# The mirrored rows of x, read backwards by plain transfers with the two halves of each third swapped

## The chip, the cores and the metric

The kernel runs on one core of a Trainium2 chip. The metric is device time in microseconds (us). Before the change the median of three runs is 629.89 us (629.77 to 629.99). The profiled execution took 629.88 us; the span that the profile covers is 628.1 us of it.

The engines of the core are named as in the profile: PE (matrix products), PEld (loads of the matrix that stays in PE), DVE, ACT and POOL (elementwise work), and SP, which only issues transfers. "SPq", "ACTq" and "POOLq" are issues and waits of an engine's instruction queue. Transfers run on 16 DMA engines.

## The reference

A two-dimensional Fourier transform of x, of which the real part is kept, goes through a gated feed-forward layer:

```python
X = np.fft.fft(x, axis=1)          # x: (8, 3008, 256)
X = np.fft.fft(X, axis=2)
x = X.real.reshape(8 * 3008, 256)
gate = np.maximum(x @ w_gate, 0.0) # 256 -> 1536
val = x @ w_val
out = gate * val @ w_out           # 1536 -> 256
```

## The kernel before, in words

With S = 3008 rows, D = 256 channels and H = S/2 = 1504, the transform along the rows is written with cosines and sines, and rows s and S - s are added or subtracted first. So each batch is loaded twice. **XD** holds rows in rising order: partition p of third t, slot q, half r of the sequence holds row 1 + 256 t + 2 p + q (+ r H). **XG** holds, on the same partitions, the pairs of rows that mirror these, in falling order. A third has 128 partitions (t = 0, 1) or 120 (t = 2), and row 0 sits beside them on partition 120 of t = 2 (`load_mirror_0`).

*How the mirrored rows come in.* For batch 0 the first third is read upwards (`load_upward`) and turned by products with a matrix `turned` (`turn`, L393, products L395); the other thirds, and all of batch 1, are fetched by a gather on POOL with an index per partition (`load_mirror`, L118). From batch 2 on, `reverse(b)` (L176) copies the rows backwards from x into a scratch tensor `xr` in DRAM, in six blocks of 64 rows, `reverse_0` (L182) adds row 0, and `load_reversed` (L186) reads `xr` into XG.

*The folds.* In batch 0, DVE adds XD and XG into AA, third by third (L461 to L478), and forms F and G. For every later batch POOL does it in `fold_steps` (L224): six `fold_a` (L198) add XD into XG, six `fold_pq` (L206) combine the halves into AA, then `fold_f` and `fold_g` write F and G. XG is free for the next batch when `fold_pq` and `small` (L251) are done. The folds of batches 1 and 2 run in one piece in batch 0 (`run_fold(99)`); those of batch b + 2 for b = 1 to 5 are spread over the tiles of batch b, 0.72 us of them for each tile.

*The tiles.* Each batch goes through PE in blocks of columns (four of 376 in batch 0, three of at most 512 later), and each block through 12 tiles of 128 hidden units. From batch 1 on, one tile (`slot`, L1030) takes a product for the sine part (L1016), its copy by ACT (L1019), a seed of the cosine part by ACT from the row block CB (L1011), a sum on DVE (L1027), a sum on POOL (L1028), the value products and the gated product h on DVE (L909). POOL executes L1028 and the fold steps in the order in which they are written. The output products (L781) of one block are spread over the tiles of the next, ACT copies each finished pair of output banks to `os` (L794, four buffers), and SP stores it to `out` (L806).

*SP's order.* SP issues in the order in which the program writes it: loads of XD (L96, L102), of XG, of CB and V, the copies of leftover columns (LB, L904), and the stores. An instruction of SP that waits holds back all behind it. `channel_loads` (L128) fetch one channel of batches 2 to 7 with 4-byte elements, into CX; `channel_turn` (L143) puts the mirrored part into a scratch tensor in DRAM backwards (L151, two blocks of 64 or 60 rows) and gets it back (L155). `wrow` and `brow` (L835, L836) carry a row of weights through DRAM to the bias of the seeds (`b2`, L837).

*The start.* SP and ACT issue the first loads, POOL and DVE build small vectors, PE and ACT build the tables of angles (`angle`, L357), POOL issues the loads of the weights (`load_w`, L341) on its software queue, and PE then transforms batch 0 (`dft_first`, L612, products L621) as its folds come in. The first tile's first product is L964.

Of the kernel before, what the change touches and what calls it, by code (L numbers as in the profile page):

```python
# [11 lines left out]
F32 = mybir.dt.float32  # L12
# [14 lines left out]
ROUND = 12582912.0  # L27
# [7 lines left out]
def kernel(  # L35
# [55 lines left out]
    pairs = x.rearrange("b (s two) d -> (b s) (two d)", two=2)  # L91

    def load_rows(b, ts=range(3)):
        for t in ts:
            n = (128, 128, 112)[t]
            nc.sync.dma_start(out=XD[0:n, :, t].rearrange("p r a d -> p r (a d)"),  # L96
                              in_=dram(x, (b * S + 1 + t * 256) * D, [[2 * D, n], [H * D, 2], [1, 2 * D]]))

    def load_last(b):
        for a in range(2):  # L100
            n = (8, 7)[a]
            nc.sync.dma_start(out=XD[112:112 + n, :, 2, a, :], in_=dram(x, (b * S + 1 + 2 * (256 + 112) + a) * D, [[2 * D, n], [H * D, 2], [1, D]]))  # L102
# [9 lines left out]
    def load_half(t, r, queue):  # L112
        queue.dma_start(out=XD[:, r, t], in_=dram(x, (1 + r * H + t * 256) * D, [[2 * D, 128], [D, 2], [1, D]]))

# [3 lines left out]
    def load_mirror(b, t, r):  # L118
        n = (128, 128, 120)[t]
        nc.gpsimd.indirect_dma_start(  # L120
            out=XG[0:n, r, t, :, :].rearrange("p a d -> p (a d)"), out_offset=None, in_=pairs,
            in_offset=bass.IndirectOffsetOnAxis(ap=gidx[0:n, 2 * t + r:2 * t + r + 1], axis=0), element_offset=b * S * D)

    def load_upward(t, r, queue):
        first = H - 128 - 128 * t - r * (H // 2)
        queue.dma_start(out=XG[:, r, t, :, :].rearrange("p a d -> p (a d)"), in_=pairs[first:first + 128, :])

    def channel_loads():  # L128
# [5 lines left out]
        for t in range(2):  # L134
            load(CX[:, 0, t], 2 * S + 1 + 256 * t, [2 * D, 128], [D, 2])
            load(CX[:, 1, t], 3 * S - H - 256 - 256 * t, [2 * D, 128], [D, 2])
        for q in range(2):
            load(CX[0:120 - q, 0, 2, q], 2 * S + 513 + q, [2 * D, 120 - q])
        load(CX[120:121, 0, 2, 1], 2 * S, [2 * D, 1])
        load(CX[0:120, 1, 2], 3 * S - H - 512 - 240, [2 * D, 120], [D, 2])  # L140
        return loads

    def channel_turn():  # L143
# [3 lines left out]
        for k, (ts, h, w) in enumerate(pieces):  # L147
# [5 lines left out]
            def get(ts=ts, h=h, cr=cr):  # L153
                for c in range(2):
                    nc.sync.dma_start(out=CX[c * h:c * h + h, 1, ts].rearrange("p t q n -> p (t q n)"), in_=cr[1 - c])  # L155
# [16 lines left out]

    PC, NC = 64, 6
    xr = nc.dram_tensor("xr", (B, 2, NC, PC, 2 * D), F32).ap()

    def reverse(b):  # L176

        for r in range(2):
            top = (H - 1 - r * (H // 2)) - NC * PC + PC
            nc.sync.dma_start(out=xr[b, 1 - r], in_=dram(x, b * S * D + top * 2 * D, [[PC * 2 * D, NC], [-2 * D, PC], [1, 2 * D]]))  # L180

    def reverse_0(b):  # L182
        for r in range(2):
            nc.sync.dma_start(out=xr[b, 1 - r, 0, 120 - PC:121 - PC, :], in_=dram(x, b * S * D + r * H * D, [[2 * D, 1], [1, 2 * D]]))

    def load_reversed(b):  # L186
        W = PC * 2 * D
        for h in range(2):
            nc.sync.dma_start(out=XG[h * PC:(h + 1) * PC].rearrange("p r t a d -> p (r t) (a d)"),
                              in_=dram(xr, (b * 2 * NC + 2 * NC - 1 - h) * W, [[2 * D, PC], [-2 * W, NC], [1, 2 * D]]))  # L190

# [32 lines left out]
    def fold_steps(b):  # L224
# [14 lines left out]
        if b + 1 < B:  # L239
            steps.append((0.0, lambda: reverse_0(b + 1) if b else None))  # L240
# [18 lines left out]
        if b + 1 < B:  # L259
            last.insert(3, (0.0, lambda: load_reversed(b + 1)))  # L260
# [956 lines left out]
```

## Time and profile before

| | us |
|---|---|
| median of three runs | 629.89 |
| profiled execution | 629.88 |
| its span | 628.1 |
| PE busy | 617.9 |
| DVE busy | 550.9 |
| POOL busy | 502.7 |
| ACT busy | 445.8 |

A row of a timeline is: start in us, duration in us, engine, source line, operation, output <- inputs, shapes, how many instructions were merged, and in brackets how long the engine was idle before and what released it. A row of the table by stretches is: its bounds, its length, then the busy time of PE, PEld, DVE, ACT and POOL with their numbers of instructions, the granted clock, the mean share of the 16 DMA engines and the GB/s that they moved. A share can exceed 1, since the records of packets in flight on one engine overlap. A group of a line or tile gives the number of instructions and the least, median and largest duration in ns.

### The profile page before, as it was taken

To read this page: it belongs to the slowest core of one execution; us is meant where nothing else is said; L and a number is where in the kernel's file an instruction comes from. 1 tells how busy PE (TensorE), PEld (TensorE's weight loads), DVE (VectorE), ACT (ScalarE), POOL (GpSimd) and SP (SyncE) were. 2 spreads that over 40 slices of the span, in tenths; PEclk is the share of its full clock that TensorE was granted. 3 is DMA by queue.
4 is the path that set the end of the run, shared out by engine and by line. 5 is a ranking of instruction groups with operands and counts; after the bars stand their busy time and mean duration, and the time that the engine had idled before them with its cause. 6 is when DMAs were issued, how large, how long until landed. Compare 5 with 4: busy or idle time off the path is not lost.

```text
span 628.1 us, 12374 instructions
## 1 busy us (share of the span) xinstructions
PE 617.9 (98%) x4057; PEld 398.2 (63%) x4102; DVE 550.9 (88%) x979; ACT 445.8 (71%) x814; POOL 502.7 (80%) x478
## 2 busy tenths in 40 slices
PE   8999999999999999999999999999999999999997
PEld 3566666666666666666666666666666666666666
DVE  8886676999899899988999999899999989999991
ACT  7796667777677767777777767777777777777762
POOL 8988992998899988799979989699886566666660
PEclk9999999999999999999999999999999999999999
DMA  9954758734263427315362326211221111211113
GB/s 240 210 201 130 169 184 106 186 66 141 86 155 137 132 70 196 101 48 161 91 185 68 131 76 138 61 52 35 76 62 37 42 60 56 60 35 50 53 50 95
DMA packets 84465, 66.47 MB, mean 106 GB/s; under 512 B 40070, under 2 KB 67494, under 8 KB 84400
## 3 DMA queue, kind: packets, MB, share of 16 engines
q1 hardware_dynamic: 79814, 60.01, 34.5%
q0 software_dynamic: 3984, 4.92, 4.0%
q8 instruction: 32, 0.52, 0.4%
q10 hardware_dynamic: 602, 0.75, 0.3%
q14 instruction: 33, 0.27, 0.1%
HBM read 41.88 MB, written 34.17 MB: 121 GB/s over the span
## 4 chain that ended last, share of the span: by engine, by line
PE 93%; DVE 3%; issue 1%; ACT 1%; DMA 1%; DVEq 0%; ACTq 0%
PE o L781 37%; PE v L874 10%; PE v L879 10%; PE g L1016 8%; PE p L1023 8%; PE v L873 8%; PE d L585 4%; DVE h L909 2%; PE p L879 1%; PE p L873 1%; PE p L874 1%; PE v L395 1%; DMA XG<-in_x_dram 1%; DVE h L898 1%; DVE r L1027 1%
## 5 line engine op out<-in xcount | busy, mean ns | idle before, releaser
L1028 POOL TENSOR_TENSOR r<-r 128x512 f32<-128x512 f32 (+1 forms) x251 | 312.8, 1252 | 100.0 <-DVE r L1027 98.9
L909 DVE SCALAR_TENSOR_TENSOR h<-r,v 128x512 bf16<-128x512 f32 (+1 forms) x502 | 317.3, 673 | 39.1 <-PE v L879 25.5
L781 PE MATMUL o<-wo,h 128*128 128x256 bf16 x2172 | 330.7, 273 | 0.0
L781 PEld LDWEIGHTS <-h 128*128 128x128 bf16 x2220 | 216.4, 97 | 112.7 <-issue 1.6
L1011 ACT ACTIVATE p<-CB,b 128x512 f32<-128x512 bf16 (+1 forms) x251 | 171.7, 684 | 73.5 <-DVE r L1027 72.6
L1019 ACT COPY r<-g 128x512 f32<-128x512 f32 (+1 forms) x251 | 144.8, 577 | 65.4 <-PE g L1016 56.8
L1027 DVE SCALAR_TENSOR_TENSOR r<-r,p 128x512 f32<-128x512 f32 (+1 forms) x251 | 168.1, 670 | 0.6 <-ACT r L1019 0.6
L874 PE MATMUL v<-V,WB 128*128 128x512 bf16 (+3 forms) x296 | 108.7, 367 | 2.2
L879 PE MATMUL v<-V,WM 128*128 128x512 bf16 (+1 forms) x252 | 94.4, 375 | 1.1 <-DVE h L909 0.7
L1016 PE MATMUL g<-V,WM 128*128 128x512 bf16 (+1 forms) x251 | 94.2, 375 | 0.2
L1023 PE MATMUL p<-U,WA 128*128 128x512 bf16 (+1 forms) x251 | 94.2, 375 | 0.0
L873 PE MATMUL v<-U,WA 128*128 128x512 bf16 (+3 forms) x254 | 92.7, 365 | 0.0
L898 DVE TENSOR_TENSOR h<-r,v 128x376 bf16<-128x376 f32 (+2 forms) x90 | 46.0, 546 | 17.3 <-PE v L879 9.1
L873 PEld LDWEIGHTS <-WA 128*128 128x128 bf16 x348 | 33.9, 97 | 39.9 <-issue 10.7
L874 PEld LDWEIGHTS <-WB 128*128 128x128 bf16 x348 | 33.9, 97 | 33.7 <-ACT WB L677 0.2
L794 ACT COPY os<-o 128x512 f32<-128x512 f32 x92 | 52.6, 571 | 3.5 <-issue 3.0
L198 POOL TENSOR_TENSOR XG<-XG,XD 128x510 f32<-128x510 f32 x42 | 52.9, 1267 | 0.6 <-DMA XG<-xr 0.6
L889 ACT ACTIVATE r<-p 128x376 f32<-128x376 f32 (+1 forms) x80 | 38.0, 486 | 17.8 <-PE p L879 9.6
L206 POOL TENSOR_TENSOR AA<-XG 128x510 f32<-128x510 f32 x42 | 45.3, 1089 | 0.0
L1016 PEld LDWEIGHTS <-WM 128*128 128x128 bf16 x251 | 24.5, 98 | 5.7 <-issue 0.3
L879 PEld LDWEIGHTS <-WM 128*128 128x128 bf16 x253 | 24.7, 98 | 3.1
L1023 PEld LDWEIGHTS <-WA 128*128 128x128 bf16 x251 | 24.5, 98 | 3.3 <-issue 0.2
(183 smaller groups left out, 412.4 us busy)
## 6 DMA issues: line engine op xcount, KB each, us to landing
out_dram<-os SPq DMA_DIRECT2D x124, 128.0 KB
xr<-in_x_dram SPq DMA_DIRECT2D x12, 768.0 KB
XG<-xr SPq DMA_DIRECT2D x12, 768.0 KB
XD<-in_x_dram SPq DMA_DIRECT2D x15, 512.0 KB
out_dram<-os SPq DMA_DIRECT2D x35, 112.0 KB
XD<-in_x_dram SPq DMA_DIRECT2D x8, 448.0 KB
CB<-ch SPq DMA_DIRECT2D x7, 376.2 KB
out_dram<-os SPq DMA_DIRECT2D x13, 96.0 KB
```

Source lines behind the costliest of these rows:

```text
L198: e.tensor_tensor(XG[p, r, t, ::-1, 1:D], XG[p, r, t, ::-1, 1:D], XD[p, r, t, :, D - 1:0:-1], op=ALU.add)
L781: nc.tensor.matmul(st["p"][0:m, q, :], lhsT=lhs(f), rhs=wo[:, f, :], start=(f == 0 and not (early and q)), stop=(f == NF - 1), skip_group_ ...
L873: nc.tensor.matmul(bank[:, 0:st["n"]], lhsT=WA[i][:, st["f"]], rhs=st["us"], start=True, stop=False)
L874: nc.tensor.matmul(bank[:, 0:st["n"]], lhsT=WB[i][:, st["f"]], rhs=st["vs"], start=False, stop=True)
L879: nc.tensor.matmul(bank[:, 0:st["n"]], lhsT=W[i][:, st["f"]], rhs=v, start=False, stop=True, skip_group_check=True)
L909: nc.vector.scalar_tensor_tensor(half_h(st, sign), in0=st["s"][1 + sign][:, 0:n], scalar=0.0, in1=st["v"][:, 0:n], op0=ALU.max, op1=ALU.mult)
L1011: nc.scalar.activation(st["p"][:, 0:st["n"]], st["c"], ACTF.Copy, scale=b2[:, st["fi"]:st["fi"] + 1])
L1016: nc.tensor.matmul(st["g"][:, 0:n], lhsT=WM[0][:, st["f"]], rhs=st["vs"], start=True, stop=True)
L1019: nc.scalar.copy(q[:, 0:n], st["g"][:, 0:n])
L1023: nc.tensor.matmul(st["p"][:, 0:n], lhsT=WA[0][:, st["f"]], rhs=st["us"], start=False, stop=True, skip_group_check=True)
L1027: nc.vector.scalar_tensor_tensor(sp[:, 0:n], in0=q[:, 0:n], scalar=-0.5, in1=st["p"][:, 0:n], op0=ALU.mult, op1=ALU.add)
L1028: nc.gpsimd.tensor_tensor(sm[:, 0:n], sp[:, 0:n], q[:, 0:n], op=ALU.add)
```

## The change

All mirrored rows are now read by plain transfers that walk backwards through x. A transfer cannot walk backwards over all partitions of a third here, so each third is cut into two halves of 64 (or 60) partitions: the outer loop of the mirror load takes the two halves in rising order, the inner loop takes the rows of a half in falling order. The mirrored rows thus stand with the two halves of each third swapped, and the rows of XD, the channel loads, and the vectors from which the tables are made (`u`, `urow`) are swapped in the same way. The turning products, the index vector and the gathers, the scratch tensor `xr` with its copies, and the special path for the first third of batch 0 go away. Some small vectors of the start move from DVE to POOL.

```diff
-    pairs = x.rearrange("b (s two) d -> (b s) (two d)", two=2)
+    HALF = (64, 64, 60)
+    def load_half(b, t, c, queue=nc.sync):
+        h = HALF[t]
+        n = 52 if (t, c) == (2, 0) else h
+        queue.dma_start(out=XD[c * h:c * h + n, :, t].rearrange("p r a d -> p r (a d)"),
+                        in_=dram(x, (b * S + 1 + t * 256 + 2 * (1 - c) * h) * D, [[2 * D, n], [H * D, 2], [1, 2 * D]]))
     def load_rows(b, ts=range(3)):
         for t in ts:
-            n = (128, 128, 112)[t]
-            nc.sync.dma_start(out=XD[0:n, :, t].rearrange("p r a d -> p r (a d)"),
-                              in_=dram(x, (b * S + 1 + t * 256) * D, [[2 * D, n], [H * D, 2], [1, 2 * D]]))
+            for c in (1, 0):
+                load_half(b, t, c)
...
-    def load_mirror(b, t, r):
-        n = (128, 128, 120)[t]
-        nc.gpsimd.indirect_dma_start(
-            out=XG[0:n, r, t, :, :].rearrange("p a d -> p (a d)"), out_offset=None, in_=pairs,
-            in_offset=bass.IndirectOffsetOnAxis(ap=gidx[0:n, 2 * t + r:2 * t + r + 1], axis=0), element_offset=b * S * D)
-    def load_upward(t, r, queue):
-        first = H - 128 - 128 * t - r * (H // 2)
-        queue.dma_start(out=XG[:, r, t, :, :].rearrange("p a d -> p (a d)"), in_=pairs[first:first + 128, :])
+    def load_mirror(b, t, r, queue=nc.sync):
+        h = HALF[t]
+        top = H - 1 - 128 * t - r * (H // 2) - h
+        queue.dma_start(out=XG[0:2 * h, r, t, :, :].rearrange("p a d -> p (a d)"),
+                        in_=dram(x, (b * S + 2 * top) * D, [[h * 2 * D, 2], [-2 * D, h], [1, 2 * D]]))
+    def load_mirrors(b):
+        load_mirror_0(b)
+        for t in range(3):
+            for r in range(2):
+                load_mirror(b, t, r)
...
-        for t in range(2):
-            load(CX[:, 0, t], 2 * S + 1 + 256 * t, [2 * D, 128], [D, 2])
-            load(CX[:, 1, t], 3 * S - H - 256 - 256 * t, [2 * D, 128], [D, 2])
-        for q in range(2):
-            load(CX[0:120 - q, 0, 2, q], 2 * S + 513 + q, [2 * D, 120 - q])
+        for t in range(3):
+            h = HALF[t]
+            for c in (1, 0):
+                for qs in ((slice(0, 1), slice(1, 2)) if (t, c) == (2, 0) else (slice(0, 2),)):
+                    m = h - (t == 2 and c == 0) * qs.start
+                    load(CX[c * h:c * h + m, 0, t, qs], 2 * S + 1 + 256 * t + 2 * (1 - c) * h + qs.start, [2 * D, m], [D, qs.stop - qs.start])
+            load(CX[0:2 * h, 1, t], 3 * S - H - 256 * t - 4 * h, [2 * D, 2 * h], [D, 2])
...
-                for c in range(2):
-                    nc.sync.dma_start(out=CX[c * h:c * h + h, 1, ts].rearrange("p t q n -> p (t q n)"), in_=cr[1 - c])
+                nc.sync.dma_start(out=CX[0:2 * h, 1, ts].rearrange("p t q n -> p (t q n)"), in_=cr.rearrange("c p n -> (c p) n"))
...
-    xr = nc.dram_tensor("xr", (B, 2, NC, PC, 2 * D), F32).ap()
-    def reverse(b):
...
-    def reverse_0(b):
...
-    def load_reversed(b):
...
-        if b + 1 < B:
-            steps.append((0.0, lambda: reverse_0(b + 1) if b else None))
...
         if b + 1 < B:
-            last.insert(3, (0.0, lambda: load_reversed(b + 1)))
-        if b + 2 < B:
-            last.append((0.0, lambda: reverse(b + 2)))
+            last.insert(3, (0.0, lambda: load_mirrors(b + 1)))
...
     for r in range(2):
-        load_upward(0, r, (nc.sync, nc.scalar)[r])
+        load_mirror(0, 0, r, (nc.sync, nc.scalar)[r])
+    for c in (1, 0):
+        load_half(0, 0, c, (nc.scalar, nc.sync)[c])
+    load_rows(0, (1,))
     for r in range(2):
-        load_half(0, r, (nc.sync, nc.scalar)[r])
-    load_rows(0, (1,))
-    load_mirror_0(0)
-    load_spare()
+        load_mirror(0, 1, r)
...
+    for k in (32, 96):
+        nc.gpsimd.memset(XD[k:k + 32, :, 2, 1, :], 0.0)
+    load_rows(0, (2,))
+    load_last(0)
+    load_mirror_0(0)
+    for r in range(2):
+        load_mirror(0, 2, r)
+    load_spare()
...
-    def turn(r):
-        p = psV.tile([128, 512], F32, name="v", tag="v")
-        nc.tensor.matmul(p[:], lhsT=turned[:], rhs=XG[:, r, 0, :, :].rearrange("p a d -> p (a d)"), start=True, stop=True)
-        upright.append(p[:].rearrange("p (a d) -> p a d", a=2))
...
     angle(1, 0)
-    turn(0)
+    spin(2)
+    angle(2, 3)
     nc.scalar.activation(ad[:], md[:], ACTF.Abs)
...
-    angle(2, 3)
-    turn(1)
     angle(3, 2)
...
     def turns_and_rows():
         load_rows(1)
         load_last(1)
-        load_mirror_0(1)
         for n, c in enumerate(even_order):
             even_turns(n, c)
             if n == 1:
                 minus_v(nc.gpsimd, 1)
-            if n:
-                load_mirror(1, (n - 1) // 2, (n - 1) % 2)
-        load_mirror(1, 2, 1)
-        reverse(2)
+        load_mirrors(1)
...
-    for at, step in zip((-5, -4, -3, -2, -1, 7, 7, 8, 14, 17), channel_loads() + channel_turn()):
+    for at, step in zip((-5, -5, -4, -3, -3, -2, -1, -1, -1, 7, 7, 14, 17), channel_loads() + channel_turn()):
```

Not shown: the swap in `u` and `urow`, and the moves from DVE to POOL (the products for `md`, the memsets of FN, CX and of XD). In batch 0 all three thirds now take one path: DVE adds XG and XD into AA as it did for the second and the third.

## The prediction

> **What bounds the kernel now.** I read the page first: busy times, the chain that ended last, the queues.
>
> ```profile
> span 628.1 us, 12374 instructions
> ...
> PE 617.9 (98%) x4057; PEld 398.2 (63%) x4102; DVE 550.9 (88%) x979; ACT 445.8 (71%) x814; POOL 502.7 (80%) x478
> ...
> PE 93%; DVE 3%; issue 1%; ACT 1%; DMA 1%; DVEq 0%; ACTq 0%
> ...
> L1028 POOL TENSOR_TENSOR r<-r 128x512 f32<-128x512 f32 (+1 forms) x251 | 312.8, 1252 | 100.0 <-DVE r L1027 98.9
> ```
>
> TensorE is busy 98% of the span and carries 93% of the chain. So nothing is gained by freeing another engine, and whatever makes PE stand is lost for good. The only part where PE is not the bound is the start, so next I read the timeline of the first 19 us.
>
> ```profile
> 0.75 0.40 SPq L126 DMA_DIRECT2D XG<-in_x_dram  x1
> ...
> 4.50 2.04 PE L395 MATMUL v<-XG,turned 128*128 128x512 f32 x2 [0.45 <-DMA XG<-in_x_dram]
> ...
> 5.18 0.48 DVE L381 MEMSET XD<- 32x512 f32 x1
> ...
> 6.83 0.67 DVE L472 TENSOR_TENSOR AA<-v,XD 128x510 f32<-128x510 f32 x1
> ...
> 6.97 1.91 PE L395 MATMUL v<-XG,turned 128*128 128x512 f32 x2
> ...
> 10.59 1.22 DVE L461 TENSOR_TENSOR AA<-XG,XD 128x1020 f32<-128x1020 f32 x1
> ...
> 13.95 1.22 DVE L461 TENSOR_TENSOR AA<-XG,XD 121x1020 f32<-121x1020 f32 x1 [0.40 <-issue]
> ...
> 18.70 0.32 PE L964 MATMUL p<-U,WA 128*128 128x376 bf16 x1
> ```
>
> The folds of the three blocks of rows (AA, t = 0, 1, 2) begin at 6.83, 10.59 and 13.95 us, and the first tile of the real work (L964) follows the third by 4.75 us. The folds need the mirrored rows XG, so a late XG moves everything behind it.
>
> **How fast a transfer with a short outer loop goes.** This decides the case, so I looked in the trace for transfers shaped like the new one. The new mirror load reads `[[h*2D, 2], [-2D, h], [1, 2D]]`: an outer loop of 2, then 64 (or 60) rows of 2 KB downwards. Two relatives run already: `reverse` (L180, outer loop 6, same rows) and the put of `channel_turn` (L151, outer loop 2, rows of 192 B). SP's timeline gives the times at which they run, and stretches in which hardly anything else moves give their rate (last three columns: granted clock, mean share of 16 DMA engines, GB/s).
>
> ```profile
> 30.07 0.60 SPq L105 DMA_DIRECT2D XG<-in_x_dram  x1
> 30.72 1.52 SPq L180 DMA_DIRECT2D xr<-in_x_dram  x2
> 32.35 3.37 SPq L835 DMA_DIRECT2D wrow<-WB  x1
> ...
> 120.30 8.69 SPq L133 DMA_DIRECT2D CX<-in_x_dram  x2
> ...
> 135.42 0.61 SPq L151 DMA_DIRECT2D cr<-CX  x1
> ```
>
> ```profile
> 30.70:33.00 2.30, 2.30 (x20) 1.69 (x19) 2.30 (x5) 1.53 (x5) 2.02 (x4) 1.00 0.10 12
> 33.00:36.00 3.00, 3.00 (x24) 2.20 (x23) 2.65 (x7) 2.80 (x7) 2.70 (x4) 1.00 0.38 147
> ...
> 136.60:137.40 0.80, 0.80 (x7) 0.49 (x5) 0.68 (x2) 0.72 (x2) 0.80 (x2) 1.00 0.15 30
> 14.00:17.00 3.00, 2.91 (x16) 1.17 (x16) 2.86 (x9) 1.29 (x8) 2.43 (x3) 1.00 1.24 200
> ```
>
> Two `reverse` transfers were issued back to back, and the share is 0.38 of 16 = 6.1 engines, not 12 and not 16: a transfer with a short outer loop runs on as many engines as that loop counts, and the second goes to the same six. Each engine moves 147/6 = 24.5 GB/s, which is 83.6 ns for a row of 2 KB. The put, with an outer loop of 2, shows 0.15 of 16 = 2.4. I take 2 engines for a mirror load; a count of 2.4 would make its time 2/2.4 of what follows. The Trainium skill, "DMA: Bandwidth & Descriptors", section "Why a DMA increments its semaphore by 16 and not by 1", gives the count as the largest number up to 16 that divides the slowest loop of both sides, and says that the hardware queues use the lowest-numbered engines; by it the count is exactly 2, the mirror loads of one batch take 31.4 us on two engines and not 26.2 us as with 2.4, and the two rows agree with it better than with any even spread.
>
> Two things more stand in these rows. Packets flow at full rate about 1.7 us after the issue (0.10 of 2.30 us is 0.6 us at 0.38). And what is issued behind such a transfer stands: L835, one small row, held SP for 3.37 us behind the two `reverse`, and L133 held it for 8.69 us behind the next two.
>
> **The change, part by part.** One mirror load is 128 rows on 2 engines: 64 x 83.6 ns = 5.35 us (5.02 us for t = 2 with 60 a side); six are 31.4 us one after the other, since all use the same two engines. A batch's set therefore ends 0.6 (`load_mirror_0`) + 1.7 + 31.4 = 33.7 us after SP issues it.
>
> *Start.* The same two engines must also pass their part of the other loads: six halves of XD, 8 rows each = 48 x 83.6 ns = 4.0 us, and of the weights. The table of queues and transfers:
>
> ```profile
> q0 software_dynamic: 3984, 4.92, 4.0%
> ...
> XG<-in_x_dram,gidx POOLq DMA_INDIRECT x10, 5.9
> ```
>
> The software queue took 4.0% of 628.1 = 25.1 us per engine; its ten gathers of 256 KB are 2.62 MB/16/24.5 GB/s = 6.7 us of it, which leaves 18.4 us, and since the records of a stretch with weights alone overlap (share 1.24), some 15 us. Sum 31.4 + 4.0 + 15 = 50.4 us, from 0.75 + 1.7: the last mirrored rows are there at about 53 us. The third fold then starts at 53 and not at 13.95: **+39 us**. Bounds: +24 us if the mirror loads are served ahead of all weights, +40 if not. I take the upper end because the queues share an engine and the weights are needed right afterwards. What the change takes out here lies under this wait: the four turning products (2.04 and 1.91 us), four gathers on POOL, the constants moved from DVE to POOL, with the new memsets of XD there (0.48 us for one on DVE at 5.18; on POOL I bound it by nothing and 2 us). Without that cover they are worth at most 2 us, the distance by which the first fold could move forward.
>
> *Batch 1's rows.* Here and below times are on the clock of before; the 39 us come on top. `load_mirrors(1)` can be issued at 30.07, when XG is free. The sets land at 32.4 + 5.35 n (+5.02): 37.7, 43.1, 48.4, 53.8, 58.8, 63.8. POOL's folds:
>
> ```profile
> 64.95 1.40 SPq L189 DMA_DIRECT2D XG<-xr  x2
> ```
>
> ```profile
> 50.11 7.39 POOL L198 TENSOR_TENSOR XG<-XG,XD 128x510 f32<-128x510 f32 x6
> ...
> 75.70 7.38 POOL L198 TENSOR_TENSOR XG<-XG,XD 128x510 f32<-128x510 f32 x6
> 83.05 0.23 POOL L230 TENSOR_TENSOR XG<-XG,XD 128x12 f32<-128x12 f32 x1
> ...
> 91.76 1.66 POOL L222 TENSOR_TENSOR G<-AA 128x762 bf16<-128x762 f32 x1
> 104.58 2.51 POOL L1028 TENSOR_TENSOR r<-r 128x512 f32<-128x512 f32 x2 [11.16 <-DVE r L1027]
> ```
>
> The sixth L198 began at 50.11 + 5 x 1.23 = 56.3; it now waits for 63.8, so this fold ends 7.5 us later. The next set is issued when XG is free again: 64.95 + 7.5 = 72.5, ends at 106.2. The sixth L198 of batch 2 was due at 81.9 and comes 24.3 us later; the fold's end moves from 93.4 to 117.7. POOL had 11.16 us to spare there, but its first L1028 was due at 104.58: batch 1's tiles start **+13 us** late. PE's waits for the transforms of batch 1, for `brow` (queued behind the first set) and for CB (behind the second) fall in the same stretch and are smaller, so I don't add them. The six gathers that POOL no longer issues bring nothing: it waited for a marker of DVE ahead of 50.11.
>
> *Batch 1 and 2.*
>
> ```profile
> 107.39 1.28 SPq L189 DMA_DIRECT2D XG<-xr  x2
> ...
> 175.00 1.34 SPq L189 DMA_DIRECT2D XG<-xr  x2
> ...
> 234.78 1.36 SPq L189 DMA_DIRECT2D XG<-xr  x2
> ```
>
> ```profile
> 135.75 1.26 POOL L198 TENSOR_TENSOR XG<-XG,XD 128x510 f32<-128x510 f32 x1
> ...
> 201.85 1.29 POOL L198 TENSOR_TENSOR XG<-XG,XD 128x510 f32<-128x510 f32 x1
> ```
>
> Issued at 107.39 the set ends at 141.1, but its last fold was due at 135.75: 5.4 us late on a POOL that is nearly full there. The set can also be issued some us earlier against the shifted tiles, so between 0 and 5.4: I take **+3**. Issued at 175.00 it ends at 208.7, due at 201.85: 6.9 us, **+7**.
>
> *Batches 3 to 5: the stores behind the mirrors.* From here the rows come in time. But stores of results go out on the same queue, and a store issued behind a set cannot finish on two of its 16 engines before the set has. The buffer `os` has four copies, each freed by its store.
>
> ```profile
> 235.93 0.58 ACT L794 COPY os<-o 128x512 f32<-128x512 f32 x1
> ...
> 253.04 0.58 ACT L794 COPY os<-o 128x512 f32<-128x512 f32 x1
> ...
> 261.85 0.58 ACT L794 COPY os<-o 128x512 f32<-128x512 f32 x1
> ```
>
> Four copies fall between 235.93 and 253.04, after the issue at 234.78; the fifth, at 261.85, needs the buffer of the first, whose store ends behind the set at 268.5 + 1. ACT stands 7.7 us; behind it are the copies of the sine part (L1019) and the seeds (L1011), which PE needs for the next tile. One tile is prepared ahead; the 251 tiles of L1028 fill the span from 104.58 on, so one is 2.1 us, so PE loses 5.5 us, three times: **+16.5**. In batch 2 the same wait lies beside POOL's, so it isn't counted again.
>
> *The rest.* The loads of XD become eight issues a batch where there were five:
>
> ```profile
> L96 SPq DMA_DIRECT2D XD<-in_x_dram x23: 318/465/499, 1.7 to 354.6; - x23
> ```
>
> That is three more at some 0.47 us, on an SP with idle time. The channel's loads are eleven where they were eight, one with 59 rows, which I can't place on engines from any row: between nothing and the 8.69 us of L133, once, and nothing taken, since it lies under the 13 us. The copies through `xr` go away: 12 x 768 KB each way, on engines that were not a bound.
>
> **Sum.** 39 + 13 + 3 + 7 + 16.5 = 78.5 us. The profiled execution took 629.88 us (span 628.1 and 1.8 around it), the median of the runs is 629.89, so both give **708 us**.
>
> **Rivals.** (1) *The later waits are absorbed.* ACT is 71% and POOL 80% busy, and stores may pass on the other 14 engines and be held less than I think. Then only start and batch 1 remain: 39 + 13, 682 us; with the lower bound of the start, 667. Against it: L835 and L133 did stand. (2) *The mirror load spreads over 16 engines after all*, for instance because its two loops are cut otherwise than those of L151. Then one set takes 6 x 8 x 83.6 ns = 4.0 us and every row is in time; the start loses the products on the chain at 4.50 and gains up to 2 us: **628 us, faster**. It turns at about 6 to 8 engines, where a set (63 us of engine time) ends in the 8 to 10 us that the start leaves. For it: L151's 0.15 is 2.4 and not 2. Against: 6.1 for an outer loop of 6. (3) *The waits add up.* ACT's wait of 7.7 us passes to PE in full, and stands beside POOL's in batch 2 (7 + 8), batch 1 pays 5.4, and `brow` costs ACT another 5 us:
>
> ```profile
> 63.66 0.19 ACT L837 CAST b<-brow 128x12 f32<-128x12 bf16 x1
> ```
>
> Its source row (L835) is issued behind the first set, which ends at 63.8; landing, a second issue and landing add some 5 us to that. Together: 39 + 13 + 5.4 + 15 + 23 + 5 = 100, **730 us**.
>
> **How the numbers follow.** My forecast 57%, rival 1 20%, rival 3 15%, rival 2 8%. The range 672 to 742 holds the first, most of rival 1 and all but the tail of rival 3; it leaves out rival 2 and the deepest absorption, some 17%. About 0.2% is what a measurement of this kernel can tell from no change; only rival 2 is faster or about equal: faster 6%, within 0.2% 2%, slower 92%.
>
> **What would show it.** Right: after the first two microseconds a long stretch with a DMA share near 0.13 and some 50 GB/s whenever mirror loads run alone; the third fold (AA, t = 2) at about 53 us and PE idle before it; POOL's L198 of batches 1 and 2 waiting for XG in steps of 5.35 us; ACT waiting for `out<-os` about once a batch in batches 2 to 5. Wrong: XG in place within some 5 us of its issue (then rival 2), or a start as said but no wait for `os` (rival 1).

## The result and the profile after

The changed kernel takes 746.27 us (median of 4 runs, 744.81 to 747.97) against 629.94 us before (629.77 to 630.14): a ratio of 1.1846, 95% interval 1.1832 to 1.1861, or 116.3 us more; the execution that the profile below shows took 747.97 us. The forecast of 708 named the direction and the mechanism, but the time lies 4 us above its range.

The page of the changed kernel (span 746.2 us): busy times, the slices of PE and of its granted clock, the software queue that carries the weights, the chain, and two groups.

```profile
span 746.2 us, 12447 instructions
...
PE 641.3 (86%) x4100; PEld 404.5 (54%) x4100; DVE 551.6 (74%) x972; ACT 445.9 (60%) x814; POOL 495.4 (66%) x477
...
PE   2228998849879996998799959997799999999998
...
PEclk9857999969989997999799989999799999999999
...
q0 software_dynamic: 3184, 2.36, 2.3%
...
PE 67%; DMA 18%; SPq 7%; POOL 4%; DVE 2%; issue 2%; ACT 1%; ACTq 0%; DVEq 0%; POOLq 0%
...
L183 POOL TENSOR_TENSOR XG<-XG,XD 128x510 f32<-128x510 f32 x42 | 53.0, 1265 | 42.8 <-DMA XG<-in_x_dram 42.8
L753 ACT COPY os<-o 128x512 f32<-128x512 f32 x92 | 52.7, 572 | 46.8 <-DMA out_dram<-os 43.6
```

PE no longer carries 93% of the chain but 67%; DMA (18%) and SP's queue (7%) took most of the rest. Two groups that hardly waited before now wait over 40 us each: POOL's folds for the mirrored rows (XG), and ACT's copies to `os` for the stores. PE is idle 104.9 us (746.2 - 641.3), where it was 10.2. And it is busy 23.4 us longer (some of it records that the trace of before lacks): the row of the granted clock has a lower digit beside nearly every slice in which PE stood.

The same kernel's timeline: SP's issues, the three folds of batch 0 on DVE (L434 is the old L461), the first tile on PE (L923), the waits of POOL (L183, the old L198; L987, the old L1028) and of ACT (L753 and L970, the old L794 and L1011).

```profile
4.45 16.44 SPq L123 DMA_DIRECT2D XG<-in_x_dram  x2
...
22.72 1.22 DVE L434 TENSOR_TENSOR AA<-XG,XD 128x1020 f32<-128x1020 f32 x1 [16.77 <-DMA XD<-in_x_dram]
43.54 1.22 DVE L434 TENSOR_TENSOR AA<-XG,XD 128x1020 f32<-128x1020 f32 x1 [17.86 <-DMA XG<-in_x_dram]
56.20 1.22 DVE L434 TENSOR_TENSOR AA<-XG,XD 121x1020 f32<-121x1020 f32 x1 [9.70 <-DMA XD<-in_x_dram]
63.16 0.52 PE L923 MATMUL p<-U,WA 128*128 128x376 bf16 x1
74.09 19.48 SPq L123 DMA_DIRECT2D XG<-in_x_dram  x6
...
130.21 1.27 POOL L183 TENSOR_TENSOR XG<-XG,XD 128x510 f32<-128x510 f32 x1 [1.85 <-DMA XG<-in_x_dram]
135.48 1.27 POOL L183 TENSOR_TENSOR XG<-XG,XD 128x510 f32<-128x510 f32 x1 [4.01 <-DMA XG<-in_x_dram]
...
150.91 1.26 POOL L183 TENSOR_TENSOR XG<-XG,XD 128x510 f32<-128x510 f32 x1 [3.58 <-DMA XG<-in_x_dram]
151.61 0.58 ACT L753 COPY os<-o 128x512 f32<-128x512 f32 x1 [6.96 <-DMA out_dram<-os]
164.17 0.69 ACT L970 ACTIVATE p<-CB,b 128x512 f32<-128x512 bf16 x1 [9.27 <-DMA CB<-ch]
170.86 2.50 POOL L987 TENSOR_TENSOR r<-r 128x512 f32<-128x512 f32 x2 [8.36 <-DVE r L986]
173.46 5.17 SPq L765 DMA_DIRECT2D out_dram<-os  x3
178.73 0.65 SPq L110 DMA_DIRECT2D XG<-in_x_dram  x1
...
251.31 0.65 SPq L110 DMA_DIRECT2D XG<-in_x_dram  x1
252.00 19.70 SPq L123 DMA_DIRECT2D XG<-in_x_dram  x6
271.81 5.63 SPq L765 DMA_DIRECT2D out_dram<-os  x2
286.29 0.58 ACT L753 COPY os<-o 128x512 f32<-128x512 f32 x1 [8.91 <-DMA out_dram<-os]
358.31 0.59 PE L975 MATMUL g<-V,WM 128*128 128x512 bf16 x1 [7.45 <-ACT r L978]
```

The third fold comes at 56.20 (it was at 13.95), the first tile at 63.16 (18.70). Two of the three folds end a wait for rows of XD and not of XG: by the forecast's sum these loads pass through the same two engines as the mirrors, and SP, held for 16.44 us by two mirror loads, issues part of them late. What each of the two adds is not separated. POOL's folds of batch 2 follow each other in steps of the transfer (130.21, 135.48). A set issued at 251.31 should end 33.7 us later, at 285.0; ACT's copy got its buffer back at 286.29.

Stretches of the same kernel: one between the third fold and the first tile, one with nothing but mirror loads, then one stop of PE in batch 3 and the time behind it (the last three columns are granted clock, share of the DMA engines, GB/s).

```profile
60.00:62.00 2.00, 2.00 (x7) 0.84 (x7) 1.18 (x3) 0.47 (x1) 0.66 (x1) 0.50 0.33 117
80.00:93.00 13.00, 12.79 (x92) 8.45 (x91) 10.24 (x21) 11.49 (x28) 1.73 (x4) 1.00 0.14 51
...
353.00:358.00 5.00, 0.00 (x0) 0.00 (x0) 0.00 (x0) 0.81 (x2) 0.21 (x1) 0.57 0.25 83
358.00:360.00 2.00, 1.69 (x7) 1.02 (x7) 0.69 (x1) 1.86 (x4) 0.94 (x1) 0.50 0.20 33
360.00:362.00 2.00, 2.00 (x7) 0.87 (x6) 0.98 (x2) 0.68 (x2) 0.32 (x1) 0.50 0.48 142
362.00:364.00 2.00, 2.00 (x9) 1.06 (x8) 0.99 (x2) 0.23 (x1) 0.93 (x1) 0.50 0.34 78
364.00:366.00 2.00, 2.00 (x15) 1.31 (x14) 1.03 (x2) 1.42 (x4) 1.56 (x2) 1.00 0.47 136
```

In the second row 0.14 of 16 engines is 2.2, at 51 GB/s: the two engines of the forecast. The lower five rows show what the forecast had not: PE stands from 350.9 to 358.31, its clock is halved meanwhile and stays halved until 364, and in those last 6 us PE is "busy" but does 7 to 9 matmuls in 2 us where the next row has 15.

Where the 118 us of the span come in. Each row is the start of one instruction in the two traces, and the shift that is new since the row above; the last column is the forecast's term.

| instruction | before | after | new | forecast |
|---|---|---|---|---|
| first tile on PE (L964, now L923) | 18.70 | 63.16 | +44.5 | 39 |
| first sum of batch 1 (L1028, now L987) | 104.58 | 170.86 | +21.8 | 13 |
| of batch 2 | 178.74 | 254.91 | +9.9 | 3 |
| of batch 3 | 250.54 | 337.55 | +10.8 | 7 |
| of batch 4 | 324.28 | 421.77 | +10.5 | 5.5 |
| of batch 5 | 397.25 | 504.44 | +9.7 | 5.5 |
| of batch 6 | 471.00 | 589.40 | +11.2 | 5.5 |
| end of span | 628.1 | 746.2 | -0.4 | 0 |

Every term but the last is in its place and was too small, by 40 us together. That leaves two questions: is it the two engines alone, and why does each stop cost more than worked out?

### The profile page after: what moved, and what is told of

It reads as the page before. It is cut to its first block, busy times and chain, and to the rows that moved or that the text cites. A ratio compares the mean times of both kernels' runs of the same rounds, so it can differ in the third digit from the quotient of the medians.

```text
span 746.2 us, 12447 instructions
## 1 busy us (share of the span) xinstructions
PE 641.3 (86%) x4100; PEld 404.5 (54%) x4100; DVE 551.6 (74%) x972; ACT 445.9 (60%) x814; POOL 495.4 (66%) x477
## 4 chain that ended last, share of the span: by engine, by line
PE 67%; DMA 18%; SPq 7%; POOL 4%; DVE 2%; issue 2%; ACT 1%; ACTq 0%; DVEq 0%; POOLq 0%
PE o L740 27%; DMA XG<-in_x_dram 10%; PE v L838 7%; PE g L975 7%; PE v L832 7%; PE v L833 7%; PE p L982 6%; DMA out_dram<-os 6%; SPq L123 4%; PE d L544 3%; DVE h L868 1%; DMA XD<-in_x_dram 1%; SPq L96 1%; POOL AA L191 1%; DMA CB<-ch 1%
## 5 line engine op out<-in xcount | busy, mean ns | idle before, releaser
L987 POOL TENSOR_TENSOR r<-r 128x512 f32<-128x512 f32 (+1 forms) x251 | 312.7, 1251 | 130.4 <-DVE r L986 126.9
L868 DVE SCALAR_TENSOR_TENSOR h<-r,v 128x512 bf16<-128x512 f32 (+1 forms) x502 | 317.7, 673 | 64.8 <-PE v L838 37.7
L740 PE MATMUL o<-wo,h 128*128 128x256 bf16 x2172 | 337.1, 276 | 0.0
L740 PEld LDWEIGHTS <-h 128*128 128x128 bf16 x2220 | 219.7, 99 | 166.0 <-issue 57.0
L970 ACT ACTIVATE p<-CB,b 128x512 f32<-128x512 bf16 (+1 forms) x251 | 171.8, 685 | 85.2 <-DVE r L986 75.2
L975 PE MATMUL g<-V,WM 128*128 128x512 bf16 (+1 forms) x251 | 96.2, 383 | 31.0 <-ACT r L978 30.9
L833 PE MATMUL v<-V,WB 128*128 128x512 bf16 (+3 forms) x296 | 110.5, 373 | 0.0
L832 PE MATMUL v<-U,WA 128*128 128x512 bf16 (+3 forms) x296 | 110.5, 373 | 0.0
L183 POOL TENSOR_TENSOR XG<-XG,XD 128x510 f32<-128x510 f32 x42 | 53.0, 1265 | 42.8 <-DMA XG<-in_x_dram 42.8
L753 ACT COPY os<-o 128x512 f32<-128x512 f32 x92 | 52.7, 572 | 46.8 <-DMA out_dram<-os 43.6
L832 PEld LDWEIGHTS <-WA 128*128 128x128 bf16 x348 | 34.3, 99 | 48.6 <-issue 19.8
L580 PE MATMUL p<-tabC,F 128*128 128x376 bf16 (+2 forms) x12 | 4.5, 513 | 40.5 <-DVE F L414 40.5
L434 DVE TENSOR_TENSOR AA<-XG,XD 128x1020 f32<-128x1020 f32 (+1 forms) x3 | 3.7, 1222 | 44.3 <-DMA XD<-in_x_dram 26.5
```

The costliest lines, as they stand in the source:

```text
L183: e.tensor_tensor(XG[p, r, t, ::-1, 1:D], XG[p, r, t, ::-1, 1:D], XD[p, r, t, :, D - 1:0:-1], op=ALU.add)
L740: nc.tensor.matmul(st["p"][0:m, q, :], lhsT=lhs(f), rhs=wo[:, f, :], start=(f == 0 and not (early and q)), stop=(f == NF - 1), skip_group_ ...
L832: nc.tensor.matmul(bank[:, 0:st["n"]], lhsT=WA[i][:, st["f"]], rhs=st["us"], start=True, stop=False)
L833: nc.tensor.matmul(bank[:, 0:st["n"]], lhsT=WB[i][:, st["f"]], rhs=st["vs"], start=False, stop=True)
L868: nc.vector.scalar_tensor_tensor(half_h(st, sign), in0=st["s"][1 + sign][:, 0:n], scalar=0.0, in1=st["v"][:, 0:n], op0=ALU.max, op1=ALU.mult)
L970: nc.scalar.activation(st["p"][:, 0:st["n"]], st["c"], ACTF.Copy, scale=b2[:, st["fi"]:st["fi"] + 1])
```

## The experiments

*Is it the number of engines?* The first run keeps the new kernel but reads the mirrored rows upwards, in one loop of 128 (so they stand in the wrong order, and the output is another one).

```diff
-  in_=dram(x, (b * S + 2 * top) * D, [[h * 2 * D, 2], [-2 * D, h], [1, 2 * D]]))
+  in_=dram(x, (b * S + 2 * (top - h + 1)) * D, [[2 * D, 2 * h], [1, 2 * D]]))
```

> The changed kernel, but every mirror load reads its 128 (or 120) pairs of rows upwards in one loop, so same bytes, same number of transfers, outer loop of 128 and not 2. The mirrored rows then stand in the wrong order, so the output is another one. Theory (a load with an outer loop of 2 runs on 2 DMA engines, and all lost time comes from that): 626 to 633 us, third fold at 13 to 16 us. Rival A (the halves of XD, the constants moved to POOL or the longer order of SP cost the time): stays above 700. Rival B (reading downwards is what is slow): also some 630, told apart by the next two.

Measured: 636.84 us, ratio 1.0105 [1.009, 1.0121]. Of 116 us, 109 went; POOL's folds wait 0.0 us for XG. The remaining 7 us lie wholly ahead of the first tile (+7.0 there, and no more behind it). That is above the 626 to 633 us expected: once the mirrors are fast, the other parts of the change cost 7 us. The second run also reads upwards, but in two loops of 64.

```diff
-  in_=dram(x, (b * S + 2 * top) * D, [[h * 2 * D, 2], [-2 * D, h], [1, 2 * D]]))
+  in_=dram(x, (b * S + 2 * (top - h + 1)) * D, [[(h - 1) * 2 * D, 2], [2 * D, h], [1, 2 * D]]))
```

> The changed kernel, rows read upwards but still as an outer loop of 2 with 64 (60) rows inside; the second half starts one pair early, so that the two loops do not join to one. Rows are in the wrong order and one pair is read twice, one left out. Theory (engines follow the outer loop): 740 to 752 us, DMA share near 0.13 where mirror loads run alone. Rival B (downward reading is slow): some 630.

Measured: 746.32 us (one execution), the time of the changed kernel. So the direction costs nothing that this shows; the outer loop of 2 costs 109 of the 116 us. The next two do the whole computation with each third cut into eight groups of 16 partitions, and into four of 32. The cut shows four groups; not shown are the loads of XD and of the channel and the tables, which follow the new order.

```diff
-    HALF = (64, 64, 60)
+    NG = 4
+    HALF = (128 // NG, 128 // NG, 120 // NG)
...
-                        in_=dram(x, (b * S + 2 * top) * D, [[h * 2 * D, 2], [-2 * D, h], [1, 2 * D]]))
+                        in_=dram(x, (b * S + 2 * top) * D, [[h * 2 * D, NG], [-2 * D, h], [1, 2 * D]]))
```

> The whole computation, rows read downwards, but each third cut into 8 groups of 16 (or 15) rows and not 2: the outer loop of a mirror load is 8, XD comes in 8 transfers a third, and the tables and channel loads follow the new order. Theory: 8 engines, a set of six takes 31.4 / 4 = 7.9 us and not 31.4; from batch 1 on all rows are in time and no store waits long; only the start is later, by 2 to 6 us, because SP issues 10 transfers a third at some 0.45 us: 630 to 640 us. Rival B (downward reading is slow): above 700. The point at which the set stops mattering was put at 6 to 8 engines in the prediction.

> The whole computation with each third cut into four groups of 32 (or 30) rows, so that the mirror load's outer loop counts 4. If the count of that loop is the number of engines, a set takes 64/4 x 83.6 ns x 6 / 2 = 15.7 us: half of the changed kernel's and twice that of eight groups. Start: rows of both kinds and weights on four engines, 15.7 + 4 + 15 + 2.5 = 37 us for the third fold (35 to 40), as in the run with eight groups, which was held by SP's issues instead. Later batches: a set issued at 64.95 (clock of before) ends at 83 and its last fold was due at 81.9, and the stores behind a set of 17.4 us come back before the fifth copy to os (26 us after the set's issue), so nothing is lost there: from batch 2 on the shift is constant. Total 660 (652 to 668). Rival, that what decides is only whether the loop walks backwards or is split, and not how many engines it counts: as slow as two groups, over 720. Rival, that stores and CB behind any set cost batches 2 to 5 something: 3 to 5 us a batch, 670 to 680.

Measured: eight groups 662.37 us, ratio 1.0512 [1.0497, 1.0526]; four groups 659.5 us, ratio 1.0474 [1.0457, 1.0492]. Stretches within a set, of eight groups and then of four:

```profile
58.00:61.00 3.00, 3.00 (x25) 2.20 (x23) 2.65 (x5) 2.81 (x8) 2.65 (x5) 1.00 0.50 187
```

```profile
63.00:69.00 6.00, 6.00 (x47) 4.21 (x45) 5.09 (x10) 5.64 (x15) 3.52 (x6) 1.00 0.26 101
```

0.50 and 0.26 of 16 are 8.0 and 4.2 engines, at 23 to 24 GB/s each. With four groups the shift is +29.1 at the first tile and +29.0 at the end of the span: from there on nothing is lost, as expected, and 4 engines are enough for a set in a batch, where the prediction had put the turn at 6 to 8. The start was not as expected: the third fold came at 41.36 us and not at 35 to 40, so the total is right in part by luck. (The 15.7 us of that expectation are half of 31.4; the product written before them gives 4.0.) Eight groups missed the number, for two reasons that their timeline of SP shows:

```profile
1.64 11.52 SPq L97 DMA_DIRECT2D XD<-in_x_dram  x14
14.05 1.28 SPq L124 DMA_DIRECT2D XG<-in_x_dram  x2
15.45 10.55 SPq L97 DMA_DIRECT2D XD<-in_x_dram  x8
...
130.49 16.69 SPq L138 DMA_DIRECT2D CX<-in_x_dram  x19
...
149.21 0.68 SPq L111 DMA_DIRECT2D XG<-in_x_dram  x1
```

XD and the channel must be read in as many pieces as there are groups, and SP issues them one by one: the last third of XD is issued only from 15.45 on, and the third fold, at 36.07, has waited 7.12 us for XD (first tile +24.2); and 19 channel loads keep the set of mirrors back to 149.21, for which POOL then waits 7.85 us (+7.3). The last run of this kind gives one engine loop of 128 to batch 0 alone; all other batches keep the halves.

```diff
+  in_=dram(x, (b * S + 2 * (top - h + 1)) * D, [[2 * D, 2 * h], [1, 2 * D]]) if b == 0 else
   dram(x, (b * S + 2 * top) * D, [[h * 2 * D, 2], [-2 * D, h], [1, 2 * D]]))
```

> The changed kernel, with the six mirror loads of batch 0 alone read upwards in one loop (wrong order of rows in batch 0); batches 1 to 7 as in the changed kernel. By the shifts in the trace of the changed kernel the start is worth 44.5 us to the first tile, the rest 73.6: theory (the terms add, the sets are independent of each other) 746 - 44.5 = 702, range 697 to 707. By the terms of the prediction (39 us for the start) 707. If the later waits depend on the start (rows of batch 1 that come earlier against the tiles), below 690.

Measured: 707.96 us (one execution), a little over the expected stretch. The first tile comes 6.8 us late instead of 44.5, so taking the two engines away from the start wins 37.7 us, and the shift from the first tile to batch 1 stays (+22.9). The 6.8 us that are left were sought with the first experiment as a base, by moving a memset of G that POOL does late, behind its issues of weights, back to DVE.

```diff
-    nc.gpsimd.memset(GG[1][:].rearrange("p i t q d -> p (i t q) d")[:, :, 0:1], 0.0)
+    nc.vector.memset(GG[1][:].rearrange("p i t q d -> p (i t q) d")[:, :, 0:1], 0.0)
```

> The run with mirror loads upwards in one loop (wrong order of rows), and one more edit: the clearing of the first column of G for batch 0, which the change had moved to POOL behind the issue of all weights (14.0 us), goes back to DVE. In the run without it PE waited 5.29 us for this clearing at 15.3 us, and the run ended 6.9 us behind the kernel before. Theory (with 16 engines for the mirror loads nothing else in the change costs anything): 628 to 632 us. If something else in the new start costs: 633 to 637.

Measured: 634.64 us, ratio 1.0069 [1.005, 1.0088]: 2.2 us of the 6.9 that the first experiment lost, by the medians. Two of the four executions took 633.4 and 633.6 us at a granted clock of 1.00, two 635.7 and 635.8 at 0.996 to 0.997, so the memset is worth between 1 and 3.4 us. PE's wait of 5.29 us for that memset is gone, and one of 2.81 us behind it has come up; in the execution traced, one of the slower two, PE then works at half clock from 21.9 us until the first tile at 25.26. Timeline of this run, the third fold:

```profile
19.01 1.22 DVE L434 TENSOR_TENSOR AA<-XG,XD 121x1020 f32<-121x1020 f32 x1 [4.55 <-DMA XD<-in_x_dram]
```

It is 5.1 us later than before the change, and waits for rows of XD although the mirrors come in one loop of 128. The last of these rows that SP issues are those of `load_spare` (L115), at 12.29 us, where the kernel before issued them at 3.42; whether that is the reason was not tried.

*What does a stop cost?* A loss per set was taken away first: the mirrors of batches 1 and 2 alone upwards, in one loop.

```diff
+  in_=dram(x, (b * S + 2 * (top - h + 1)) * D, [[2 * D, 2 * h], [1, 2 * D]]) if b in (1, 2) else
   dram(x, (b * S + 2 * top) * D, [[h * 2 * D, 2], [-2 * D, h], [1, 2 * D]]))
```

> The changed kernel with the mirror loads of batches 1 and 2 alone read upwards in one loop, so on 16 engines (their rows come in the wrong order: the output is not the reference's). If the losses add up by the set that causes them, the shift from the first tile to batch 1's first sum (21.8 us in the changed kernel: stores and CB behind set 2, and folds of sets 1 and 2 waiting for XG) goes and all else stays: 746.3 - 21.8 = 724.5 (720 to 728). If a loss is only moved (set 3 can then be issued earlier against the tiles and stops something else): over 732. If set 1 or 2 also cause part of batch 1's own 9.9 us: under 718.

Measured: 722.82 us (one execution; 724.5 expected). The shift is the same at the first tile and at batch 1's first sum (+44.0 at both), so all of the 21.8 us belongs to sets 1 and 2. Then `os` got six buffers instead of four, with ten of `r` instead of twelve to pay for them.

```diff
-                    os_ = rp.tile([128, 2, D], F32, name="os", tag="os", bufs=4)
+                    os_ = rp.tile([128, 2, D], F32, name="os", tag="os", bufs=6)
...
-        return rp.tile([128, 512], F32, name="r", tag="r", bufs=12)
+        return rp.tile([128, 512], F32, name="r", tag="r", bufs=10)
```

> The changed kernel with six buffers os for results where there were four; the room comes from the pool r, ten buffers where there were twelve. All loads as in the changed kernel. Theory (stores stand behind a set of mirror loads, ACT waits for the buffer of the first store, PE stops, and the granted clock halves after the stop): two more buffers cover two more copies at some 5.7 us, 11 us, more than the waits of 8.3 to 9.2 us; the waits of ACT for os in batches 3 to 5 and the one in batch 0 go, batch 2 keeps POOL's wait: 746 less three times 10.5 and less 3 to 10 in batches 0 and 2, that is 702 to 713 us, and PE busy falls from 641 by some 9 us or more, since fewer products run at half clock. Rival (PE's stops come from late rows or from the order of SP, not from os): 740 or more.

Measured: 722.02 us, ratio 1.1457 [1.1438, 1.1477]: 24 us better than the change, where more was expected. The copies to `os` wait 3.2 us in all instead of 46.8, and PE is busy 636.0 us instead of 641.3. Batches 3 and 4 then lose next to nothing (+0.7 and 0.0), so their 10.5 and 9.7 us came from the wait for `os` alone, with the half clock behind it; batch 2 keeps 6.5 of its 10.8, POOL's part. Batch 5 gains 2 us and the start of batch 1 nothing. What stands there, in this run's timeline:

```profile
164.58 0.69 ACT L970 ACTIVATE p<-CB,b 128x512 f32<-128x512 bf16 x1 [16.93 <-DMA CB<-ch]
...
505.80 3.69 SPq L863 DMA_DIRECT2D LB<-h  x6
507.60 0.27 PE L740 MATMUL o<-wo,LB 128*128 128x256 bf16 x1 [1.18 <-DMA LB<-h]
```

In batch 0 the wait for `os` is gone and the next one, for CB, has grown from 9.27 to 16.93 us: the same late end, another last step. In batch 5 PE takes up the wait itself, for the leftover columns LB, which SP issues behind the set of mirrors: six such waits of 0.8 to 1.2 us, 6.1 us together. Two waits stood side by side there, and taking one away shows the other.

The last two measure the stop by itself, in the kernel before, where no mirror load is: 28 (or 14) idle copies on ACT in one tile of batches 3, 4 and 5, before its copy of the sine part.

```diff
+                    if b in (3, 4, 5) and at == 29:
+                        cx = CX[:].rearrange("p k t q n -> p (k t q n)")
+                        for _ in range(28):
+                            nc.scalar.copy(cx, cx)
```

> The kernel before, unchanged but for 28 copies of 144 numbers on ACT (in place, on a buffer that is no longer read) in one tile of each of the batches 3, 4 and 5: at an estimated 0.3 us a copy a stop of ACT of some 8.4 us, as long as the waits for os in the changed kernel, with all transfers as before. By the prediction's way of counting (one tile of 2.1 us is prepared ahead, the rest is lost, and nothing more) 3 x 6.3 = 19: 649 us, PE busy unchanged at 618. If a stop also costs the clock: 3 x (6.3 + 3 to 4), 658 to 661 us, PE busy 627 to 630, granted clock of the run near 0.95 to 0.96.

> As the run before, with 14 copies: a stop of ACT of some 4.2 us. Without a cost in clock 3 x 2.1 = 6: 636 us. If so short a stop also costs the clock 3 to 4 us each: 645 to 648 us. A result at 636 with the longer stop at 658 or more would say that a stop has to have a certain length before the clock goes down.

Measured: 661.22 us with 28 copies, ratio 1.05 [1.0482, 1.0517], 10.4 us for each of the three stops (661.22 - 629.92, by 3); 644.49 us with 14, ratio 1.0234 [1.0217, 1.0251], 4.9 us for each. The first stop with 28 copies, as ACT and PE show it, and stretches around it:

```profile
313.13 9.55 ACT L1173 COPY CX<-CX 128x144 f32<-128x144 f32 x28
...
323.19 0.56 PE L1016 MATMUL g<-V,WM 128*128 128x481 bf16 x1 [8.08 <-ACT r L1019]
```

```profile
315.00:323.00 8.00, 0.11 (x2) 0.00 (x0) 0.71 (x2) 7.31 (x24) 1.96 (x2) 0.70 0.72 188
323.00:325.00 2.00, 1.81 (x7) 1.01 (x7) 0.66 (x1) 2.00 (x5) 1.09 (x1) 0.50 0.40 154
325.00:327.00 2.00, 2.00 (x8) 1.04 (x7) 1.19 (x2) 0.24 (x1) 0.11 (x1) 0.50 0.63 236
327.00:329.00 2.00, 2.00 (x10) 1.12 (x9) 0.69 (x2) 1.13 (x2) 1.20 (x1) 0.64 0.44 146
```

And the first and the second stop with 14 copies (PE stands 3.29 us in both, until 318.73 and until 395.14), stretches:

```profile
315.00:318.00 3.00, 0.44 (x4) 0.24 (x3) 1.03 (x2) 2.72 (x10) 2.28 (x2) 1.00 1.08 200
319.00:321.00 2.00, 2.00 (x16) 1.36 (x15) 1.21 (x3) 1.78 (x4) 1.20 (x1) 1.00 0.43 160
...
395.00:397.00 2.00, 1.86 (x8) 1.14 (x8) 0.66 (x1) 2.00 (x5) 1.14 (x1) 0.59 0.47 115
397.00:399.00 2.00, 2.00 (x8) 1.00 (x7) 1.42 (x3) 0.20 (x1) 0.06 (x1) 0.56 0.13 13
```

Of ACT's 9.55 us PE stands 8.08: only 1.5 us are covered. The lowest clock in any stretch is 0.50, so a stretch at 0.70 is read as one that was at half clock for 0.30/0.5 of its time; so the rows give 4.8 + 4.0 + 1.4 = 10.2 us at half clock, and PE, which works in the last 5.2 of them (from 323.19), loses 2.6. The batch's shift is +10.8, which is 8.08 + 2.6. With 14 copies the first stop leaves the clock at 1.00 (shift +3.4) and the second halves it for 1.6 + 1.8 = 3.4 us (+5.1): the same stop costs 1.7 us more when the clock is halved. The six stops differ: by the batches' shifts those with 28 copies cost 10.8, 9.9 and 10.7 us, those with 14 copies 3.4, 5.1 and 5.0.

## Why the prediction was right or wrong

*Right: the mechanism.* An outer loop of 2 puts a transfer on two engines. The shares 0.14, 0.26 and 0.50 for 2, 4 and 8, the steps of 5.3 us in POOL's folds, and a set's end within 1.3 us of the one worked out (285.0 against 286.29) say so, and the second experiment excludes the walk backwards as a cause. The rule of the Trainium skill, "DMA: Bandwidth & Descriptors", section "Why a DMA increments its semaphore by 16 and not by 1", by which the slowest loop sets the number of engines, agrees at these three counts. Rival 2 (16 engines after all) fell; even its price was wrong, since with one loop of 128 the new start loses 7 us and gains none of the "up to 2".

*The start, +39 against 44.5.* Two terms were too small. The third fold came at 56.20 us where 53 was forecast: 3.2 us of engine time too few. By the shares, the two engines worked on until then (in stretches from 34 to 46 and from 50 to 56 us the share is 0.12 to 0.15, in the next it is 0.02). The sum had cut the weights' 18.4 us per engine to 15; the page of the changed kernel gives their queue 2.3% of 746.2, that is 17.2 us. That would be 2.2 of the 3.2, and the rest is not separated. And the first tile followed the third fold by 6.96 us where 4.75 was taken, because PE worked at half clock there (0.50 in the row 60 to 62). What the change moves in the start was put "at most 2 us" without the cover of that wait, and this was wrong as well: in the first experiment it loses 7 us. But in the changed kernel it stays covered, as forecast: POOL's memset of G, for which PE waited 5.29 us in the first experiment, is done at 14.24 us, and the first fold comes at 22.72.

*Batch 1's rows, +13 against 21.8.* POOL's last fold of batch 2 came 24.5 us later than the first tile's shift (150.91 - 81.9 - 44.5), where 24.3 was forecast, and POOL's folds ended at 162.50 (117.7 + 44.5 = 162.2 by the forecast). POOL then stood idle for 8.36 us ahead of the first sum of batch 1, which is all but 0.4 of the 8.8 us missing. The step that failed is the one after it: "PE's waits for the transforms of batch 1, for `brow` ... and for CB ... are smaller, so I don't add them". ACT's wait for `os` (6.96) and then for CB (9.27) end at 164.17, after POOL's folds, and CB is the last step ahead of batch 1. With more buffers for `os` the start of batch 1 did not move, and without sets 1 and 2 the whole 21.8 went. Whether CB was late on the two engines or on SP's queue stays open. The price of rival 3 for `brow` was not met either: ACT waited 2.3 us for it, not 5.

*Batches 1 and 2, +3 and +7 against 9.9 and 10.8.* For batch 1 the set was assumed to be issued as early as before or earlier against the tiles. SP issued it at 178.73, which is 5.0 us later than 107.39 moved by 66.3, straight after three stores that had held it from 173.46 on. A set issued later than before was outside the bounds given. PE stood 6.8 us in batch 1, above the 5.4 that was its upper bound, and half clock adds 3.4. For batch 2 POOL's part comes near the 7 forecast (6.5 with six buffers), but by luck: PE then stands 4.5 us for h, and half clock adds 1.7. And ACT's wait for `os` (8.91) does not lie wholly beside it, as I had said: with four buffers PE stands 6.7 us behind ACT and 1.4 for h.

*Batches 3 to 5, 16.5 against 31.4.* The wait for `os` is where and of the size that was forecast: 8.27, 9.10 and 9.24 us for "7.7". The sum then took off a tile "prepared ahead", 2.1 us. PE stood 7.45, 8.30 and 8.42 us of these, so 0.8 is covered each time, and 1.5 in the bare experiment. Half clock adds 2.8, 1.5 and 2.5 us.

*What no term had.* The sum puts the clock at nothing. But at a stop, and for some us after it, PE's clock is often halved, for 3.4 us or a multiple of it. Its size is read from the second experiment, which takes the same time and whose page holds about as many matmul records as that of before (4055 and 4057; the changed kernel's has 4100):

```profile
span 744.5 us, 12402 instructions
...
PE 636.9 (86%) x4055; PEld 404.4 (54%) x4100; DVE 551.5 (74%) x972; ACT 445.9 (60%) x814; POOL 495.3 (67%) x477
```

PE is busy 19.0 us longer than before and idle 97.4 us longer. So some 19 of the 116 us are work at half clock, about half of the 38 that the forecast lacks. The trace of the changed kernel agrees: half of PE's busy time in its stretches at half clock is 2.7 us between 53.4 and 63.6, and 3.4, 3.4, 2.4, 2.8, 1.5 and 2.5 us in the six rows of the table behind the first tile. Rival 3, in which the waits add up to 100 us, comes nearest, and with 19 for the clock it would have come to 749. That this meets 746 is partly luck: batch 2 lost 10.8 us and not its 15, batch 1 9.9 and not its 5.4, and CB, not `brow`, held ACT. Its chance of 15% was too low: I had given most of these waits a cover that no row showed.

## What to carry to other kernels

Look at the outermost loop of a transfer before its direction or its bytes: here 2 halves instead of 4 groups cost 87 us, and one loop of 128 instead of 4 groups would have saved nothing more in the steady part, while more pieces on the other loads cost SP's time. Count for each transfer also what stands behind it on the queue: stores, and through their buffers ACT and PE. And when PE is the bound and is made to stand for some 3 us or more, allow for the half clock: 0 to 2.8 us for each stop here, by its length and by when it falls.

## What the runs showed of the hardware that was not expected

The clock is halved in whole steps. PE's stop of 3.29 us left 0 or 3.4 us at half clock, that of 8.08 us left 10.2 (by the stretches quoted; the first and the second stop of the one, the first of the other). The Trainium skill, "TensorE: Matmul & The Clock Gate", section "Part 1: The HAM clock gate (the "warmup" mystery)", has a window of about 3.4 us that runs freely, half rate after an idle one and full rate after a busy one. The traces agree with the length and with the free phase. By the rows quoted the half clock of the second stop with 14 copies begins at 395.36; 23 steps of 3.413 us (10.24 by 3) back lies 316.86, in the middle of the first stop (315.44 to 318.73), so that neither of the two windows there was idle for over 1.9 us. But an idle window need not be idle throughout: the stops of 3.29 us, and the one of 2.81 us in the run with the memset on DVE, are shorter than 3.4 us, and half clock followed, while the wait of 5.29 us in the first experiment left the clock at 1.00.

A transfer on few engines also holds the queue that issues it. Six mirror loads kept SP for 19.48 us with two engines (timeline above), and for less with four groups, eight groups and one loop. From the timelines of four groups, eight groups and one loop, in this order:

```profile
59.24 7.15 SPq L124 DMA_DIRECT2D XG<-in_x_dram  x6
```

```profile
53.95 4.03 SPq L124 DMA_DIRECT2D XG<-in_x_dram  x6
```

```profile
72.64 2.81 SPq L123 DMA_DIRECT2D XG<-in_x_dram  x6
```

So the stores behind a set were late twice: at SP, which reached them 20 us later (271.81 after 252.00), and at the two engines. How much of each stop is due to the one and to the other was not separated. No run shows either whether one loop could walk backwards over a whole third, which the description of the change rules out here. Nor was a start as before joined with four groups for the later batches; since four groups lose and gain nothing behind the first tile, an estimate for it is the time of before.
